# Two attentions on one core: the first segment's output projection in half units with a PSUM bank of their own, and three banks for the maxima

## The chip, the cores and the metric

The kernel runs on one core of a Trainium2 chip. The metric is the device time of one execution in microseconds. The kernel before takes 2726.04 us, the median of three runs (2725.89 to 2726.05).

## What is computed

Two attention layers see the same input `A_x`, 2048 rows of 576 (`B_x` is drawn but not used). A has 32 heads of 18 with keys and values of their own, B has 32 query heads that share one key head and one value head. Their outputs are mixed by a gate per row. All is float32.

```python
x = A_x
g = sigmoid((x * gate_w).sum(-1, keepdims=True))
q, k, v = (x @ A_wqkv).reshape(1, S, 3, H, Dh).transpose(2, 0, 3, 1, 4)   # H = 32, Dh = 18
a = (softmax(q @ k.T * Dh ** -0.5) @ v).transpose(0, 2, 1, 3).reshape(1, S, D) @ A_wo
q = (x @ B_wq).reshape(1, S, H, Dh).transpose(0, 2, 1, 3)
b = (softmax(q @ (x @ B_wk).T * Dh ** -0.5) @ (x @ B_wv)).transpose(0, 2, 1, 3).reshape(1, S, D) @ B_wo
return g * a + (1 - g) * b
```

## The kernel before

**Heads and steps.** The 64 heads (B's 32 first, then A's) are worked through one after the other, each in 16 steps. A step `T` takes one tile of 128 keys against all 2048 queries. The loop at L797 writes out two steps at a time; such a pair is the unit of time in what follows, and a head is eight pairs. Before the loop come the projections (all products that make q, k and v, in split float32), and 11 pairs of lead with negative `T`.

**What a step does.** Scores are `k` times `q` over 54 rows (high and low halves in float16) and two rows that subtract the row maximum; four matmuls of 512 queries each (`step_scores`, L548), in the order strings "sA0" to "sA3" for the first step of the pair and "sB0" to "sB3" for the second. ScalarE turns each into exponentials (L555). One or two steps later `step_pv` (L561) multiplies these by the values and adds into the accumulator `acc`, which has a PSUM bank to itself: "P" or "Q" for all 512 columns of a group, "p", "f", "h", "H" for halves of 256. After a head's last step `head_out` (L571) copies `acc` out with VectorE.

**The maxima.** They are found 22 steps ahead (`LEAD`) by the same product in the other orientation, in other rows of the TensorE array, so a maximum and a score run side by side. Per pair there are eight such matmuls (`step_max`, L511): "mA2", "mA0", "mA3", "mB0" to "mB3", and "x". For "x" the keys' difference of two blocks is used; ScalarE takes its relu (L514), and VectorE adds that to "mA0" of the following pair (L517), which spares "mA1". All the others are reduced by VectorE (L520).

**Order.** The engines run what they are given in program order. `manual_schedule` is on, so the order of the calls is the order of the queues. It is written out by hand in strings, one per kind of pair, L789 to L795:

```python
    PLAIN = "sA0 mA2 sA1 mA0 sA2 mA3 P sA3 mB0 sB0 mB1 sB1 mB2 h sB2 mB3 sB3 x H"
    UNIT = "sA0 mA2 sA1 mA0 sA2 mA3 P sA3 mB0 sB0 mB1 sB1 mB2 U sB2 mB3 sB3 x Q"
    END = "sA0 mA2 sA1 mA3 sA2 mB0 P sA3 mB1 sB0 mA0 sB1 x Q sB2 mB2 sB3 mB3"
    AFTER = "sA0 mA2 p sA1 mA0 sA2 mA3 sA3 x f sB0 mB0 sB1 mB1 h sB2 mB2 sB3 mB3 H"
```

UNIT is taken whenever a unit of the output projection is due; otherwise END where `T` is a multiple of 16, AFTER behind an END, and PLAIN. ALONE stands for the last 11 pairs, which have no maxima left.

**PSUM.** Eight banks: `ps_s` has three for scores, `ps_m` four, `ps_o` one for `acc`. A pool hands its banks out in turn; a tile's first writer waits until the readers of the tile that had the bank are done. `ps_m` serves the maxima (of "x" too), the units of the output projection, half of the projections ahead of the loop, and small transposes.

**The output projection** runs inside the loop, in three segments (`SEG`, L769) of 32 units each. A unit (`out_proj`, L673) is 128 rows by 288 columns: 12 matmuls with four tiles of heads and three products of high and low halves in the first two segments, 3 matmuls in the third. In the first segment ScalarE copies a unit to `oacc` (L683); in the others VectorE adds it (L685). `oih` and `oil`, the normalised heads, are loaded from DRAM by SP's queue, a pair of tiles for four units. The generator yields after each unit, and "U" in the string runs it on by one (`pull`). When units are due is said by `due`: in the first segment by the table `at_ends`, 21 of them at every 16th step from 528 and 11 at every 32nd from 522; in the second, units spread evenly over steps 942 to 1007, about one a pair.

Of the kernel before, what the change touches and what calls it, by code (L numbers as in the profile page):

```python
# [49 lines left out]
def gated_mix_kernel(ctx: ExitStack, tc: tile.TileContext, xT, wall, wv, wo, out):  # L50
# [7 lines left out]
    fixed = ctx.enter_context(tc.tile_pool(name="fixed", bufs=1, side="left"))  # L58
    dram = ctx.enter_context(tc.tile_pool(name="dram", bufs=1, space=DRAM))
    ps_s = ctx.enter_context(tc.tile_pool(name="ps_s", bufs=3, space=PSUM))  # L60
    ps_m = ctx.enter_context(tc.tile_pool(name="ps_m", bufs=4, space=PSUM))
    ps_o = ctx.enter_context(tc.tile_pool(name="ps_o", bufs=1, space=PSUM))
    ctx.enter_context(tc.manual_schedule())

# [19 lines left out]
    ones = fixed.tile([P, 32], F16, name="ones")  # L84
    ones_r = dram.tile([2, S], F16, name="ones_r")
    acc = ps_o.tile([P, 512], F32, name="acc")

    nc.vector.memset(acc, 0.0)
    nc.vector.memset(vb, 1.0)
# [68 lines left out]
    dma(mask_r, mask_d.rearrange("g (m p) -> m g p", p=P), nc.gpsimd)  # L158

    def turn_mask():  # L160
        pt = ps_m.tile([P, 512], F32, name="pm")
        for g in range(4):
            nc.tensor.transpose(pt[:, MT * g:MT * g + MT], mask_r[:, g, :], ident[0:MT, 0:MT])
        nc.vector.tensor_copy(mask, pt[:, 0:4 * MT].rearrange("p (g m) -> p g m", m=MT))
# [28 lines left out]
    def balance(g):  # L193

        r = wpool.tile([P, 2], F32, name="br", bufs=1)
        if g == 0:
            nc.vector.tensor_reduce(r, norm_b, axis=AX.X, op=OP.max)
        else:
            r0 = q_row(H) - 4 * P
            sizes = norm_a[:, r0:r0 + 2 * DH * H].rearrange("p (h a d) -> p a h d", a=2, d=DH)  # L200
            for i in range(2):
                nc.vector.tensor_reduce(r[:, i:i + 1], sizes[:, 1 - i], axis=AX.XY, op=OP.max)
        yield
        pt = ps_m.tile([P, 512], F32, name="pm")
        nc.tensor.transpose(pt[0:2, 0:P], r, ident)
        x = wpool.tile([2, 1], F32, name="bx", bufs=1)
        nc.vector.tensor_reduce(x, pt[0:2, 0:P], axis=AX.X, op=OP.max)
        nc.vector.tensor_scalar(x, x, 1e-18, 1e18, op0=OP.max, op1=OP.min)
        dg = wpool.tile([2, 2], F32, name="bd", bufs=1)
        nc.vector.tensor_scalar(dg, ident[0:2, 0:2], x, None, op0=OP.mult)  # L210
        yield
        pb = ps_m.tile([P, 512], F32, name="pm")
        nc.tensor.matmul(pb[:, 0:2], two, dg, start=True, stop=True)
        b = wpool.tile([P, 2], F32, name="bb", bufs=1)
        nc.vector.reciprocal(b[:, 1:2], pb[:, 1:2])
        nc.vector.tensor_tensor(b[:, 0:1], pb[:, 0:1], b[:, 1:2], op=OP.mult)
        e = wpool.tile([P, 2], I32, name="be", bufs=1)
        nc.vector.tensor_single_scalar(e[:, 0:1], b[:, 0:1].bitcast(I32), 24, op=OP.logical_shift_right)
        nc.vector.tensor_scalar(e[:, 1:2], e[:, 0:1], 1.0, 64.0, op0=OP.mult, op1=OP.add)
        nc.vector.tensor_scalar(e[:, 0:1], e[:, 0:1], -1.0, 190.0, op0=OP.mult, op1=OP.add)  # L220
        t = wpool.tile([P, 2], F32, name="bt", bufs=1)
        nc.vector.tensor_single_scalar(t.bitcast(I32), e, 23, op=OP.logical_shift_left)
        nc.vector.tensor_scalar(t, t, LIFT, None, op0=OP.mult)
        for i in range(2):
            nc.vector.scalar_tensor_tensor(tv, mask[:, g + i, :], t[:, i:i + 1], tv, op0=OP.mult, op1=OP.add)
# [45 lines left out]

    def shared_v(c):
        st = ST.pop(c)
        pv = ps_m.tile([P, 512], F32, name="pm")
        for j in range(4):
            nc.tensor.transpose(pv[:, 18 * j:18 * j + 18],
                                st[ROW_VB:ROW_VB + 18, j * P:(j + 1) * P],
                                ident[ROW_VB:ROW_VB + 18, ROW_VB:ROW_VB + 18])
        nc.vector.tensor_copy(vb[:, 4 * c:4 * c + 4, 0:18],
                              pv[:, 0:72].rearrange("p (j d) -> p j d", d=18))  # L280
# [215 lines left out]

    MX = {}

    def step_max(u, i, c, low=False):

        if u not in MX:
            MX[u] = mxs[u] if u < 2 else mxs[2 + u % 3]
        b = SB if low else MB
        if c == "x":
            k = L["kd", u if u >= H else 0][b:b + 54, :]
        else:
            k = kst(u)[b:b + 54, c * 512:(c + 1) * 512]
        pm = ps_m.tile([P, 512], F32, name="pm")  # L510
        nc.tensor.matmul(pm, qs[u % 3][b:b + 54, i * P:(i + 1) * P], k, start=True, stop=True)  # L511
        if c == "x":
            MX["x", u, i] = lead.tile([P, 512], F32, name="xb", bufs=2)
            nc.scalar.activation(MX["x", u, i], pm, AF.Relu)  # L514
        elif c == 0 and ("x", u, i) in MX:
            junk = lead.tile([P, 512], BF16, name="junk", bufs=1)
            nc.vector.tensor_tensor_reduce(junk, pm, MX.pop(("x", u, i)), 1.0, -3e38, op0=OP.add, op1=OP.max,  # L517
                                           accum_out=MX[u][:, i, c:c + 1])
        else:
            nc.vector.tensor_reduce(MX[u][:, i, c:c + 1], pm, axis=AX.X, op=OP.max)  # L520
# [126 lines left out]
    def out_proj(t0, rows, first=False):  # L647
# [18 lines left out]
        for q in range(8):  # L666
# [3 lines left out]
            for s2 in range(2):  # L670
                st_ = 2 * q + s2
                for hf in range(2):
                    fp = ps_m.tile([P, 512], F32, name="pm")  # L673
                    n = 0
                    for a, b in PRODS:
                        for t, r in enumerate(rows):
                            nc.tensor.matmul(fp[:, 0:288], o[b][:r, t, s2 * P:(s2 + 1) * P],  # L677
                                             w[a][:r, t, 288 * hf:288 * hf + 288],
                                             start=(n == 0), stop=(n == 3 * nt - 1))
                            n += 1  # L680
# [23 lines left out]
    def last_out():  # L704
# [6 lines left out]
        for j in range(4):  # L711
# [1 line left out]
            dma(stk[0:18, cs], oh[32 * j:32 * j + 18, :])  # L713
            dma(stk[18:36, cs], oh[32 * j:32 * j + 18, :])
            dma(stk[36:54, cs], ol[32 * j:32 * j + 18, :])
        pt = ps_m.tile([P, 512], F32, name="pm")
# [7 lines left out]
        yield  # L724
        for st_ in range(16):
            for hf in range(2):
                ps = ps_m.tile([P, 512], F32, name="pm")
# [45 lines left out]
    when(980, lambda: slow.append(prep_last()))  # L773


    at_ends = list(range(528, 849, 16)) + list(range(522, 843, 32))
    assert len(at_ends) == 32

    def due(T, t0, t1, n):
        if t0 == SEG[0][3]:  # L780
            return at_ends.count(T)
        return (n * (T - t0 + 1)) // (t1 - t0) - (n * (T - t0)) // (t1 - t0) if t0 <= T < t1 else 0

    vunits = [(st_, hf) for hf in range(2) for st_ in range(16)]
# [12 lines left out]
    for T in range(-LEAD, NSTEP + 2, 2):  # L797
# [11 lines left out]
        for op in order.split():  # L809
# [6 lines left out]
                if M + 2 < NSTEP:  # L816
                    step_max(*divmod(M + 2, 16), "x")
            elif k in "mM":
                step_max(*divmod(M + second, 16), int(c), k == "M")
            elif k == "s":  # L820
                if T < NSTEP:
                    step_scores(*divmod(T + second, 16), int(c), alone)
# [8 lines left out]
        if slow and M % 16:  # L831
            for _ in range(2 if T > 1000 else 1):
                if slow:
                    try:
                        next(slow[0])
                    except StopIteration:
                        slow.pop(0)
    while slow:
        run(slow.pop(0))
    tail = last_out()  # L840
# [37 lines left out]
```

## Time and profile before

| | us |
|---|---|
| median of three runs (lowest, highest) | 2726.04 (2725.89, 2726.05) |
| the profiled execution | 2726.16 |
| its span in the profile | 2724.3 |
| TensorE busy (matmul) | 2689.0 |
| VectorE busy | 2421.9 |
| ScalarE busy | 2389.5 |
| GpSimd busy | 285.7 |
| mean granted TensorE clock | 0.995 |

Times in the profile are microseconds from the start of the span. A busy TensorE isn't a TensorE at its peak, since matmuls overlap and their ends are modelled. The loop's step 0 has its first exponential at about 307 us; the steps with units of the first segment lie from 1485 to 2262 us, those of the second from 2479 us on.

### The profile page before, as it was taken

What the parts mean: (1) busy time and instruction counts of PE and PEld (TensorE: products, weight loads), DVE (VectorE), ACT (ScalarE), POOL (GpSimd) and SP (SyncE); (2) the same over time, 40 slices, a digit from 0 to 9 for tenths busy, and PEclk for the clock granted to TensorE, in tenths of its full rate; (3) what the DMA queues carried; (4) which work ended last, traced back from release to release, by engine and by line L of the source; (5) the groups of instructions that cost most, each with busy time, mean ns of one, the idle gap of its engine ahead of it and who ended that gap; (6) DMA issues with size and microseconds to landing.
All of it is one profiled execution on the core that took longest, in us unless ns stands there. A gap on an engine that the chain in (4) does not pass through costs nothing.

```text
span 2724.3 us, 57935 instructions
## 1 busy us (share of the span) xinstructions
PE 2689.0 (99%) x22210; PEld 957.2 (35%) x22210; DVE 2421.9 (89%) x4589; ACT 2389.5 (88%) x4809; POOL 285.7 (10%) x531
## 2 busy tenths in 40 slices
PE   8999999999999999999999999999999999999999
PEld 6767522222222222222222333333333332223444
DVE  6335899999999999999999999999999999998865
ACT  4332599999999999999999999999999999998875
POOL 3641000001000200110110001000100021001000
PEclk9999999999999999999999999999999999999998
DMA  6322100002001100110132113112221112122312
GB/s 188 114 97 85 38 16 19 20 22 59 27 18 32 45 26 17 45 43 20 32 72 80 41 49 97 40 41 57 72 66 48 47 58 64 39 68 85 89 36 95
DMA packets 127089, 150.36 MB, mean 55 GB/s; under 512 B 55339, under 2 KB 94411, under 8 KB 125614
## 3 DMA queue, kind: packets, MB, share of 16 engines
q1 hardware_dynamic: 113628, 121.86, 15.8%
q0 software_dynamic: 7968, 19.23, 2.1%
q10 hardware_dynamic: 5216, 5.57, 0.6%
q8 instruction: 174, 2.85, 0.4%
q14 instruction: 103, 0.84, 0.1%
HBM read 90.89 MB, written 46.45 MB: 50 GB/s over the span
## 4 chain that ended last, share of the span: by engine, by line
ACT 50%; PE 40%; DVE 6%; DMA 2%; issue 1%; SPq 1%; POOL 0%; DVEq 0%; ACTq 0%; POOLq 0%
ACT pt L555 45%; PE acc L561 13%; PE ps L548 11%; ACT xb L514 6%; PE pm L677 4%; PE ps L240 4%; PE pm L240 4%; DVE mx L520 3%; PE ps L289 3%; PE pm L511 1%; SPq L56 1%; DMA R<-r_d 1%; DVE oe L571 1%; DVE junk L517 1%; DVE oacc L731 0%
## 5 line engine op out<-in xcount | busy, mean ns | idle before, releaser
L555 ACT ACTIVATE pt<-ps 128x512 f32<-128x512 f32 x4052 | 2093.2, 637 | 67.8 <-PE pm L511 59.8
L520 DVE TENSOR_REDUCE mx<-pm 128x1 f32<-128x512 f32 x3096 | 1941.4, 683 | 93.6 <-PE pm L511 52.8
L548 PE MATMUL ps<-qs,ksb 56*128 56x512 f16 x2688 | 818.4, 380 | 10.7
L511 PE MATMUL pm<-ksb,qs 54*128 54x512 f16 x2364 | 742.2, 383 | 2.2 <-DVE mx L520 1.1
L561 PE MATMUL acc<-pt,vb 128*19 128x512 f32 (+1 forms) x6136 | 592.2, 458 | 1.9
L561 PE MATMUL acc<-pt,vg 128*19 128x256 f32 (+1 forms) x5664 | 579.5, 481 | 2.3 <-DVE oe L571 0.5
L511 PEld LDWEIGHTS <-qs 54*128 54x128 f16 x4096 | 332.2, 93 | 245.6 <-issue 196.7
L548 PE MATMUL ps<-qs,ksa 56*128 56x512 f16 x1364 | 404.3, 379 | 4.8 <-ACT pt L555 1.3
L548 PEld LDWEIGHTS <-ksb 56*128 56x128 f16 x2688 | 175.0, 94 | 622.1 <-issue 575.8
L511 PE MATMUL pm<-ksa,qs 54*128 54x512 f16 x1232 | 384.8, 382 | 0.5 <-ACT xb L514 0.2
L517 DVE CUSTOM_DVE_ANT_0 junk<-pm,xb 128x512 bf16<-128x512 f32 x500 | 340.6, 681 | 0.0
L514 ACT ACTIVATE xb<-pm 128x512 f32<-128x512 f32 x500 | 316.6, 633 | 0.0
L548 PEld LDWEIGHTS <-ksa 56*128 56x128 f16 x1408 | 89.3, 94 | 328.8 <-issue 298.1
L530 POOL TENSOR_SCALAR mt<-mt 128x32 f32<-128x32 f32 x64 | 18.6, 290 | 1612.0 <-DVE mt L528 1612.0
L561 PEld LDWEIGHTS acc<-pt,vb 128*19 128x19 f32 x6136 | 104.1, 96 | 223.5 <-issue 206.4
L561 PEld LDWEIGHTS acc<-pt,vg 128*19 128x19 f32 x5664 | 96.1, 97 | 222.8 <-issue 204.9
L511 PE MATMUL pm<-kdb,qs 54*128 54x512 f16 x372 | 141.5, 380 | 0.0
L248 ACT ACTIVATE ph<-ps,tv 128x512 f16<-128x512 f32 x29 | 19.8, 686 | 67.3 <-PE ps L240 43.2
L292 ACT ACTIVATE vst<-ps 128x288 f32<-128x288 f32 x32 | 13.2, 412 | 67.4 <-PE ps L289 67.4
L571 DVE COPY oe<-acc 128x512 f32<-128x512 f32 x63 | 43.6, 692 | 30.0 <-PE acc L561 27.9
L248 ACT ACTIVATE ph<-pm,tv 128x512 f16<-128x512 f32 x27 | 18.4, 686 | 54.5 <-PE pm L240 40.6
L254 DVE SCALAR_TENSOR_TENSOR pl<-pm,tv,ph 128x512 f16<-128x512 f32 x27 | 20.1, 749 | 48.8 <-ACT ph L248 38.7
(151 smaller groups left out, 1518.6 us busy)
## 6 DMA issues: line engine op xcount, KB each, us to landing
qs<-qkh SPq DMA_DIRECT2D x244, 72.0 KB
qs<-qkl SPq DMA_DIRECT2D x122, 72.0 KB
onh<-oh SPq DMA_DIRECT2D x32, 256.0 KB
onl<-ol SPq DMA_DIRECT2D x32, 256.0 KB
oih<-onh SPq DMA_DIRECT2D x16, 512.0 KB
oil<-onl SPq DMA_DIRECT2D x16, 512.0 KB
ot<-oe SPq DMA_DIRECT2D x220, 36.0 KB
R<-r_d SPq DMA_DIRECT2D x55, 144.0 KB
```

Of the source, the lines that this page charges most:

```text
L240: nc.tensor.matmul(fp[:, a0:b0], w[a][:kr, k, :], X[b][:kr, k, s0 + a0:s0 + b0], start=(n == 0), stop=(n == len(PROJ) - 1), skip_group_che ...
L248: nc.scalar.activation(h, fp, AF.Copy, scale=t)
L289: nc.tensor.matmul(fp[:, 0:288], X[b][:kr, k, st_ * P:(st_ + 1) * P], w[a][:kr, k, :], start=(n == 0), stop=(n == len(PROJ) - 1))
L511: nc.tensor.matmul(pm, qs[u % 3][b:b + 54, i * P:(i + 1) * P], k, start=True, stop=True)
L514: nc.scalar.activation(MX["x", u, i], pm, AF.Relu)
L517: nc.vector.tensor_tensor_reduce(junk, pm, MX.pop(("x", u, i)), 1.0, -3e38, op0=OP.add, op1=OP.max, accum_out=MX[u][:, i, c:c + 1])
L520: nc.vector.tensor_reduce(MX[u][:, i, c:c + 1], pm, axis=AX.X, op=OP.max)
L548: nc.tensor.matmul(ps, kst(u)[b:b + 56, i * P:(i + 1) * P], qs[u % 3][b:b + 56, c * 512:(c + 1) * 512], start=True, stop=True)
L555: nc.scalar.activation(pt, ps, AF.Exp, scale=SCALE / LIFT ** 2)
L561: nc.tensor.matmul(acc[32 * j:32 * j + 19, a:b], v_of(u, i), PT[u, i, j][:, a:b], start=(i == 0 and a == 0), stop=(i == 15), skip_group_ch ...
L571: nc.vector.tensor_copy(oe, acc)
L677: nc.tensor.matmul(fp[:, 0:288], o[b][:r, t, s2 * P:(s2 + 1) * P], w[a][:r, t, 288 * hf:288 * hf + 288], start=(n == 0), stop=(n == 3 * nt ...
```

## The change

- `ps_m` has three banks instead of four; the fourth is a pool of its own, `ps_x`.
- `side()` takes that bank. The units of the first two segments go there, and so do the small transposes ahead of the loop.
- `four()` takes `ps_m` three times and `ps_x` the fourth time. The maxima of the lead (T < 0) use it, and from step 1018 on (`L["tail"]`) the units of the third segment and what comes after the last head. The maxima from step 0 on take `ps_m` alone, and so do the first two scores of a step in the last pairs.
- The generator of the first segment yields once more, after six of a unit's twelve matmuls. Its table, `pieces`, has 64 entries from 524 to 870, 5.5 steps apart on average, for 32 units of two pieces.

```diff
-    ps_m = ctx.enter_context(tc.tile_pool(name="ps_m", bufs=4, space=PSUM))
+    ps_m = ctx.enter_context(tc.tile_pool(name="ps_m", bufs=3, space=PSUM))
+    ps_x = ctx.enter_context(tc.tile_pool(name="ps_x", bufs=1, space=PSUM))
...
+    turn = {"n": 0}
+
+    def side():
+        return ps_x.tile([P, 512], F32, name="px")
+
+    def four():
+
+        turn["n"] += 1
+        return side() if turn["n"] % 4 == 0 else ps_m.tile([P, 512], F32, name="pm")
...
-    def step_max(u, i, c, low=False):
+    def step_max(u, i, c, low=False, lead_on=False):
...
-        pm = ps_m.tile([P, 512], F32, name="pm")
+        pm = four() if lead_on else ps_m.tile([P, 512], F32, name="pm")
...
-                    fp = ps_m.tile([P, 512], F32, name="pm")
+                    fp = four() if "tail" in L else side()
                     n = 0
                     for a, b in PRODS:
                         for t, r in enumerate(rows):
+                            if first and n == 6:
+                                yield
...
-    at_ends = list(range(528, 849, 16)) + list(range(522, 843, 32))
-    assert len(at_ends) == 32
+    pieces = [524 + 11 * i // 4 * 2 for i in range(64)]
 
     def due(T, t0, t1, n):
         if t0 == SEG[0][3]:
-            return at_ends.count(T)
+            return pieces.count(T)
...
-                step_max(*divmod(M + second, 16), int(c), k == "M")
+                step_max(*divmod(M + second, 16), int(c), k == "M", T < 0)
...
+        if T >= NSTEP - 6:
+            L["tail"] = True
```

In `turn_mask`, `balance` and `shared_v` the tile comes from `side()`, in `last_out` from `four()`. By the added lines L548, L555, L511, L514, L520, L561, L571, L677 and L683 become L559, L566, L522, L525, L531, L572, L582, L690 and L696.

TensorE's queue at the start of a plain pair, in a head of B, before. A row gives the line, the operation, the tile written and the tiles read, and the semaphore of the engine waited for; `ps` is a score, `pm` a maximum, `acc` the accumulator:

```order
L548 MATMUL ps_10063<-qs0_92,ksb_95 128x512 [waits Activation_49]
L511 LDWEIGHTS qs1_93
L511 MATMUL pm_10067<-ksb_95,qs1_93 128x512 [waits DVE_49]
L548 LDWEIGHTS ksb_95
L548 MATMUL ps_10071<-qs0_92,ksb_95 128x512 [waits Activation_49]
L511 LDWEIGHTS qs1_93
L511 MATMUL pm_10075<-ksb_95,qs1_93 128x512 [waits DVE_49]
L561 MATMUL acc_100<-pt_9988,vb_97 19x512
```

The same place with the change:

```order
L559 MATMUL ps_10066<-qs0_95,ksb_98 128x512 [waits Activation_49]
L522 LDWEIGHTS qs1_96
L522 MATMUL pm_10070<-ksb_98,qs1_96 128x512 [waits DVE_49]
L559 LDWEIGHTS ksb_98
L559 MATMUL ps_10074<-qs0_95,ksb_98 128x512 [waits Activation_49]
L522 LDWEIGHTS qs1_96
L522 MATMUL pm_10078<-ksb_98,qs1_96 128x512 [waits Activation_49]
L572 MATMUL acc_103<-pt_9991,vb_100 19x512
```

The order of the instructions is the same. The last maximum ahead of `acc` (mA3) waited for VectorE and now waits for ScalarE.

TensorE's queue at a unit of the first segment, before (`woh` and `wol` are the weights' halves, `oih` and `oil` those of the heads):

```order
L548 MATMUL ps_22034<-qs2_94,ksa0_2732 128x512 [waits Activation_49]
L511 LDWEIGHTS qs1_93
L511 MATMUL pm_22038<-ksb_95,qs1_93 128x512 [waits DVE_49]
L677 MATMUL pm_22045<-woh_19342,oih_21768 128x288 [waits DMAHW7_49,DVE_49,Pool_49]
L677 MATMUL pm_22045<-woh_19342,oih_21768 128x288 [waits Pool_49] x3
L677 MATMUL pm_22045<-woh_19342,oil_21770 128x288 [waits DMAHW0_49]
L677 MATMUL pm_22045<-woh_19342,oil_21770 128x288 x3
L677 MATMUL pm_22045<-wol_19343,oih_21768 128x288 x3
L677 MATMUL pm_22045<-wol_19343,oih_21768 128x288 [waits Pool_49]
L548 LDWEIGHTS ksa0_2732
```

With the change, the second piece of a unit:

```order
L559 MATMUL ps_22712<-qs0_95,ksa1_2736 128x512 [waits Activation_49]
L522 LDWEIGHTS qs2_97
L522 MATMUL pm_22716<-ksa0_2735,qs2_97 128x512 [waits DVE_49]
L690 MATMUL px_22496<-woh_19345,oil_21773 128x288 x2
L690 MATMUL px_22496<-wol_19346,oih_21771 128x288 x4
L559 LDWEIGHTS ksa1_2736
```

Twelve matmuls in a row, into a tile of the maxima's banks, are now six, into a tile of `ps_x`.

More of the change, by code (lines that the diff above doesn't have):

```diff
@@ L160, in turn_mask @@
     def turn_mask():
-        pt = ps_m.tile([P, 512], F32, name="pm")
+        pt = side()
         for g in range(4):
@@ L203, in balance @@
         yield
-        pt = ps_m.tile([P, 512], F32, name="pm")
+        pt = side()
         nc.tensor.transpose(pt[0:2, 0:P], r, ident)
@@ L211, in balance @@
         yield
-        pb = ps_m.tile([P, 512], F32, name="pm")
+        pb = side()
         nc.tensor.matmul(pb[:, 0:2], two, dg, start=True, stop=True)
@@ L273, in shared_v @@
         st = ST.pop(c)
-        pv = ps_m.tile([P, 512], F32, name="pm")
+        pv = side()
         for j in range(4):
@@ L715, in last_out @@
             dma(stk[36:54, cs], ol[32 * j:32 * j + 18, :])
-        pt = ps_m.tile([P, 512], F32, name="pm")
+        pt = four()
         for c in range(4):
@@ L726, in last_out @@
             for hf in range(2):
-                ps = ps_m.tile([P, 512], F32, name="pm")
+                ps = four()
                 nc.tensor.matmul(ps[:, 0:288], stk[0:54, st_ * P:st_ * P + P],
```

## The prediction

> **What bounds the kernel now.** I read the page first, then the chain of waits, then the timeline of one pair of steps. The page:
>
> ```profile
> ACT pt L555 45%; PE acc L561 13%; PE ps L548 11%; ACT xb L514 6%; PE pm L677 4%; PE ps L240 4%; PE pm L240 4%; DVE mx L520 3%; PE ps L289 3%; PE pm L511 1%; SPq L56 1%; DMA R<-r_d 1%; DVE oe L571 1%; DVE junk L517 1%; DVE oacc L731 0%
> L555 ACT ACTIVATE pt<-ps 128x512 f32<-128x512 f32 x4052 | 2093.2, 637 | 67.8 <-PE pm L511 59.8
> L520 DVE TENSOR_REDUCE mx<-pm 128x1 f32<-128x512 f32 x3096 | 1941.4, 683 | 93.6 <-PE pm L511 52.8
> ```
>
> 45% of the chain that ended last is the exponential (L555) on ScalarE, 6% the relu (L514) on the same engine. TensorE is 99% busy by the page, but its ends are modelled, so the chain decides. In the middle of a head it runs on ScalarE alone:
>
> ```profile
> 1330.13 0.49 ACT xb L514
> 1330.62 3.92 ACT pt L555 x8
> 1334.54 0.49 ACT xb L514
> 1335.03 3.92 ACT pt L555 x8
> 1338.95 0.49 ACT xb L514
> ```
>
> A pair of steps is nine ScalarE instructions, eight exponentials and a relu: 3.92 + 0.49 = 4.41 us. The relu is the last of a pair. A longer pair therefore needs a loop that passes through ScalarE and is longer than 4.41 us. The timeline of the same pair:
>
> ```profile
> 1334.42 0.61 ACT L514 ACTIVATE xb<-pm 128x512 f32<-128x512 f32 x1
> 1334.59 0.37 PE L548 MATMUL ps<-qs,ksb 56*128 56x512 f16 x1
> 1334.60 0.39 PE L511 MATMUL pm<-ksb,qs 54*128 54x512 f16 x1
> 1334.89 4.05 ACT L555 ACTIVATE pt<-ps 128x512 f32<-128x512 f32 x8
> 1334.91 1.05 PE L561 MATMUL acc<-pt,vb 128*19 128x512 f32 x8
> 1335.90 0.39 PE L548 MATMUL ps<-qs,ksb 56*128 56x512 f16 x1
> 1336.13 0.38 PE L548 MATMUL ps<-qs,ksb 56*128 56x512 f16 x1
> 1336.55 0.37 PE L548 MATMUL ps<-qs,ksb 56*128 56x512 f16 x1
> 1336.56 0.39 PE L511 MATMUL pm<-ksb,qs 54*128 54x512 f16 x1
> 1336.87 0.63 PE L561 MATMUL acc<-pt,vb 128*19 128x256 f32 x8
> 1337.43 0.39 PE L548 MATMUL ps<-qs,ksb 56*128 56x512 f16 x1
> 1337.97 0.63 PE L561 MATMUL acc<-pt,vb 128*19 128x256 f32 x8
> 1338.83 0.61 ACT L514 ACTIVATE xb<-pm 128x512 f32<-128x512 f32 x1
> ```
>
> In the names of the order strings: relu of the last pair (1334.42), sA2 and mA3 side by side (1334.59), P (1334.91), sA3 (1335.90), sB0 (1336.13), sB1 and mB2 (1336.55), h (1336.87), sB2 (1337.43), H (1337.97), relu (1338.83). Two narrower looks at ScalarE give the distance of two exponentials:
>
> ```profile
> 1335.37 1.13 ACT L555 ACTIVATE pt<-ps 128x512 f32<-128x512 f32 x2
> 1335.85 1.14 ACT L555 ACTIVATE pt<-ps 128x512 f32<-128x512 f32 x2
> ```
>
> They start 0.48 apart (1334.89, 1335.37, 1335.85). Nine are 4.30, so a pair has about 0.11 of idle ScalarE, and it lies before the exponential of sB2.
>
> **The three banks.** A maximum waits until the reader of the tile that had its bank is done. With four banks that is the tile four back, with three the tile three back. A plain pair takes tiles in the order A2 A0 A3 B0 B1 B2 B3 x. mA3 is now three behind the x of the pair before, so it waits for that relu. TensorE's queue runs in order, and behind mA3 stand P, sA3 and all later scores. Before, the wait on the relu fell on mB0, which comes after P, long after the relu's end.
>
> What that does: the relu of 1334.42 ends at 1335.03, and mA3 ran at 1334.60, so mA3 comes some 0.49 later, and P and sA3 with it. sA3 has no room: it ran at 1335.90 and its exponential, the fourth of the eight, at 1335.85 + 0.48 = 1336.33, 0.43 behind. The relu of the pair comes after that exponential and four others, and the next mA3 waits for it: a loop of one pair. Its length:
>
> - the relu, 0.61;
> - from the end of a ScalarE instruction to the matmul that waited for it, 0.06: the exponential of 1335.85 with the mean of 637 ns ends at 1336.49, and sB1 waited for it until 1336.55;
> - mA3 to P, 1334.60 to 1334.91: 0.31;
> - P to sA3, 1334.91 to 1335.90: 0.99;
> - sA3 to its exponential: at least the matmul's 0.39, at most the 0.43 seen; I take 0.42;
> - five exponentials to the next relu, 5 x 0.478: 2.39.
>
> Sum 4.78, against 4.41: **+0.37 a pair**. Low end 4.74 (0.03 less for the score, 0.01 of rounding). High end 4.89, if the 0.11 of idle ScalarE ahead of sB2 stays. It should go: that idle arises because sB1 waits from 1336.35 to 1336.55 for an exponential that in the new pair is long done, so sB2 comes 1.53 - 0.20 = 1.33 after sA3, and its exponential could start 1.33 + 0.42 = 1.75 after sA3, while ScalarE gets there at 0.42 + 3 x 0.48 = 1.86. Slack 0.11.
>
> Is another three-bank wait worse? x now waits for the reduce of B1, and H and mA2 stand behind x. That loop is 0.06 + 0.31 + H to sA0 (0.56, 1337.97 to 1338.53, as h to sB2) + 0.42 + four VectorE instructions of 0.60 + a reduce of 0.68 = 4.43. It is shorter than 4.78, so it doesn't decide.
>
> How often: in the program's order 500 maxima now wait for a relu, 446 of them directly ahead of a P; before it was 8. About 30 of the 446 lie in the second segment (below). 416 x 0.37 = **+154 us** (low 416 x 0.33 = 137, high 416 x 0.48 = 200).
>
> The other 54 are in the pairs behind a head's end, where x comes before f and four more exponentials follow its relu. They cost between nothing and 0.37 each, 0 to 20. I take +5, near the bottom, because the relu ends early there.
>
> **The units of the first segment.** One of them now:
>
> ```profile
> 1575.45 0.39 PE L511 MATMUL pm<-ksa,qs 54*128 54x512 f16 x1
> 1575.76 0.56 PEld L677 LDWEIGHTS pm<-woh,oih 128*128 128x128 f32 x4 [0.23 <-issue]
> 1576.79 0.58 PEld L677 LDWEIGHTS pm<-wol,oih 128*128 128x128 f32 x4
> 1577.54 0.39 PE L548 MATMUL ps<-qs,ksa 56*128 56x512 f16 x1
> 1577.64 0.41 ACT L683 ACTIVATE oacc<-pm 128x288 f32<-128x288 f32 x1 [0.78 <-PE pm L677]
> 1577.96 1.09 ACT L555 ACTIVATE pt<-ps 128x512 f32<-128x512 f32 x2
> 1578.08 1.05 PE L561 MATMUL acc<-pt,vg 128*19 128x512 f32 x8
> ```
>
> Twelve matmuls hold TensorE between mB2 (1575.45) and sB2 (1577.54); ScalarE idles 0.78 and then copies the unit out, 0.32 to the next exponential. What a unit costs in all is read from the heads: one copy of acc each.
>
> ```profile
> L571 DVE COPY oe<-acc x32: 691/692/693, 349.7 to 1463.9; 128x512 f32<-128x512 f32 x32
> L571 DVE COPY oe<-acc x22: 691/692/692, 1503.4 to 2298.1; 128x512 f32<-128x512 f32 x22
> ```
>
> Without units a head is (1463.9 - 349.7) / 31 = 35.94; with them (2298.1 - 1503.4) / 21 = 37.84. 21 heads x 1.90 hold 30 of the units, so one costs 1.33, and 32 cost **43**. That goes.
>
> A half unit in its place: weight loads stand (1576.79 - 1575.76) / 8 = 0.129 apart, so six matmuls fewer take 0.77 off. mB2 to sB2 becomes 2.09 - 0.77 = 1.32 where a plain pair has 0.87 (1336.56 to 1337.43): +0.45. Slack 0.11 covers part, so the exponential of sB2 comes 0.34 late. In every second piece the copy (0.32) falls into just this gap: its data are ready 1577.64 - 1575.76 - 0.77 = 1.11 behind the first weight load and so 0.75 + 1.11 = 1.86 behind sA3, just when ScalarE gets there. So both kinds cost about 0.33, a unit 0.66, 32 units **+21** (0 if the gap is absorbed, 43 if halving brings nothing).
>
> Such pairs end in Q instead of H, 0.43 longer. The cover is the relu's wait: sB2 to sA0 is 1.52 there (0.23 + 0.31 + 0.98) and sA0 to mA3 0.47, together 1.99, while the relu releases mA3 at 0.42 + 2 x 0.48 + 0.61 + 0.06 = 2.05 behind sB2. Without that cover it would be 0.43 x 64 = 28. The unit's own bank waits for a copy two pairs old: nothing. The loads of oih and oil on SP's queue keep their number; they now precede the first piece of every fourth unit, and the reads they wait for are a piece's distance old. The q rows behind them in that queue are used two heads (72 us) later, and the queue is held for a piece's distance at most, 2.75 pairs or 13 us. Without the cover each of the eight pairs of loads would hold a head's first score for those 13.
>
> **The second segment** is bound by TensorE:
>
> ```profile
> 2532.86 0.60 ACT L514 ACTIVATE xb<-pm 128x512 f32<-128x512 f32 x1
> 2533.43 0.38 PE L548 MATMUL ps<-qs,ksa 56*128 56x512 f16 x1
> 2533.44 0.38 PE L511 MATMUL pm<-ksb,qs 54*128 54x512 f16 x1
> ```
>
> mA3 at 2533.44 would wait for the relu's end at 2533.46 plus 0.06: 0.08 a pair, 30 pairs, **+3**. The projections, the lead and the tail keep four banks in turn or have a bank aside: 0.
>
> Sum against the profiled execution: 154 + 5 - 43 + 21 + 3 = **+140**. That execution took 2726.16 (span 2724.3) beside the median of 2726.04, so the time is **2866**.
>
> **The rivals.** *The wait is absorbed at the heads' ends.* From the relu before a head's last pair (order END) to the relu of the third pair on there are the loop's parts up to sA3's exponential, 4.78 - 2.39 = 2.39, and then 23 ScalarE instructions; without any idle time 2.39 + 23 x 0.478 = 13.38, which is three pairs of 4.46, hardly more than today. Then a head costs 5 x 4.78 + 13.38 = 37.28, +1.4, 59 heads +83, with the units -43 + 21 and +3: 2790. For it: the two pairs without a wait could catch up. Against it: the catching up must pass TensorE, which has little idle time.
>
> *Faster.* If TensorE came to mA3 at least 0.49 later than now without ScalarE waiting, the bank would be free, and only the units would count: 2726 - 43 + 21 = 2704. For it: the trace has no plain pair where mA3 meets a busy bank. Against it: a later mA3 means a later sA3, and sA3's exponential follows it at 0.43 today, with no room. From 0.01 us of delay on, ScalarE waits.
>
> *The clock falls.* TensorE would now stand still 0.4 us in each pair, and the granted clock could drop:
>
> ```profile
> 1334.90:1339.31 4.41, 4.37 (x42) 1.28 (x40) 4.27 (x10) 4.41 (x11) 0.00 (x0) 1.00 0.01 4
> 2656.00:2672.00 16.00, 14.98 (x137) 3.63 (x138) 2.29 (x4) 14.93 (x32) 0.00 (x0) 1.00 0.07 17
> ```
>
> The last number but two is the granted clock, the second the busy TensorE. At half the clock P alone takes 0.99 more, 446 x 0.99 = +440: 3170 or more. Against it: from 2656 to 2672 TensorE idled 1.02 us in 16 and kept 1.00. The Trainium skill, TensorE: Matmul & The Clock Gate, "A second HAM failure mode: psum-queue depth-cycling", says that idling briefly as a kernel cycles through PSUM banks lets the clock oscillate; by that rule this rival holds. No run here shows it, and the row above speaks against it.
>
> **How the numbers follow.** Forecast, the relu's loop in every plain pair: 0.90. Absorbed at the heads' ends: 0.05. Faster: 0.03. Clock: 0.02. The forecast's own range: low 137 + 0 - 43 + 0 + 2 = +96, high 200 + 20 - 43 + 43 + 5 = +225. The low end has every term low at once, and the high end needs the idle ahead of sB2 to stay, which its slack speaks against, so I go from +106 to +170: **2832 to 2896**. That leaves out the rivals and the outermost tenth of the forecast. A measurement of this kernel tells 0.2% (5.5 us) from no change. Faster by more: 0.03. Within: 0.01. Slower: 0.96.
>
> **What would show it.** In plain pairs the distance of two relus is 4.78; mA3's matmul starts about 0.06 behind the end of the relu before, no longer beside sA2; ScalarE idles about 0.48 ahead of the fourth exponential of a pair and not ahead of the seventh. Heads without units take 38.1 to 38.6. Pairs with a piece take 5.1, and no copy (L683's successor) is preceded by 0.78 of idle time. Wrong it is if mA3 starts beside sA2 at the old distance, if the pairs' length hasn't changed, or if the loss lies at the heads' ends.

## The result, and the profile after

| | before | after |
|---|---|---|
| median, us (lowest, highest), four runs each | 2725.97 (2724.91, 2726.05) | 2868.72 (2868.24, 2869.99) |
| ratio, 95% interval | | 1.0525 (1.0507, 1.0544) |
| profiled execution / its span | 2726.16 / 2724.3 | 2869.08 / 2867.2 |
| TensorE busy (matmul) | 2689.0 | 2833.8 |
| ScalarE busy | 2389.5 | 2429.7 |
| mean granted TensorE clock | 0.995 | 0.994 |

The change makes the kernel 5.25% slower. One execution of the sixth experiment's kernel took 8358.23 us (it is among the four of the median given there): a score's matmul has a mean of 1.03 us in its trace and 0.38 in that of the same kernel's second run, at a mean granted clock of 1.000 and 0.995.

The page of the kernel after: the chain by line, and the two groups whose idle time grew.

```profile
PE acc L572 36%; PE ps L559 34%; PE pm L522 11%; PE px L690 4%; PE ps L251 4%; PE pm L251 3%; PE ps L300 3%; ACT pt L566 1%; DVE mx L531 1%; DVE oacc L744 0%; DVE oacc L698 0%; DVE oe L582 0%; SPq L56 0%; DMA R<-r_d 0%; ACT xb L525 0%
L566 ACT ACTIVATE pt<-ps 128x512 f32<-128x512 f32 x4052 | 2133.6, 621 | 190.9 <-PE pm L522 180.1
L531 DVE TENSOR_REDUCE mx<-pm 128x1 f32<-128x512 f32 x3074 | 1959.8, 684 | 203.6 <-PE pm L522 176.0
```

The exponential held 45% of the chain before and now holds 1%. ScalarE's idle time ahead of the exponentials grew from 67.8 to 190.9 us, VectorE's ahead of the reduces from 93.6 to 203.6, and both mostly end at a maximum (`pm`, L522), since scores and maxima run side by side. Both engines now stand waiting for TensorE, yet TensorE has no more work: it too waits. The chain of waits in the middle of a head (start, length, engine, tile and line) shows where:

```profile
1409.56 0.37 PE pm L522
1409.93 0.99 PE acc L572 x8
1410.92 0.32 PE ps L559
...
1414.37 0.37 PE pm L522
```

Before, the chain stayed on ScalarE here. Now a maximum stands in it alone for 0.37, and then the PV matmuls P for 0.99. The next such maximum comes 1414.37 - 1409.56 = 4.81 later. The chain reports the loop on TensorE's rows, although the loop passes through ScalarE; that shows only in the timeline of the same pair:

```profile
1404.75 0.37 PE L522 MATMUL pm<-ksb,qs 54*128 54x512 f16 x1
1405.05 1.05 PE L572 MATMUL acc<-pt,vb 128*19 128x512 f32 x8
1406.04 0.39 PE L559 MATMUL ps<-qs,ksb 56*128 56x512 f16 x1
1406.46 2.56 ACT L566 ACTIVATE pt<-ps 128x512 f32<-128x512 f32 x5 [0.29 <-PE pm L522]
1408.87 0.64 ACT L525 ACTIVATE xb<-pm 128x512 f32<-128x512 f32 x1
1409.14 0.38 PE L559 MATMUL ps<-qs,ksb 56*128 56x512 f16 x1
1409.56 0.37 PE L522 MATMUL pm<-ksb,qs 54*128 54x512 f16 x1
```

mA3 (1404.75), P (1405.05), sA3 (1406.04), its exponential and four more (1406.46), the relu (1408.87), and the next mA3 at 1409.56, 0.05 behind the relu's end at 1409.51. sA2 ran at 1409.14; mA3 no longer runs beside it.

The copies of `acc` (L582), one a head, for the heads without units and then for those with units of the first segment:

```profile
L582 DVE COPY oe<-acc x32: 691/692/692, 355.3 to 1547.4; 128x512 f32<-128x512 f32 x32
L582 DVE COPY oe<-acc x21: 690/692/693, 1587.7 to 2380.7; 128x512 f32<-128x512 f32 x21
```

(1547.4 - 355.3) / 31 = 38.45 a head, 35.94 before; (2380.7 - 1587.7) / 20 = 39.65, 37.84 before. The first difference is +2.51, the second +1.81. So the loss is made in heads that have no unit at all, and in the heads with units the halving takes part of it back.

The whole span, cut at the heads' first exponentials:

| stretch | before | after | difference |
|---|---|---|---|
| up to head 0 | 307.2 | 310.4 | +3.2 |
| head 0 | 39.4 | 41.6 | +2.2 |
| heads 1 to 31 | 1114.1 | 1192.1 | +78.0 |
| heads 32 to 53 (first segment) | 834.2 | 871.3 | +37.1 |
| heads 54 to 58 | 180.2 | 193.4 | +13.2 |
| heads 59 to 61 (second segment) | 139.7 | 145.3 | +5.6 |
| heads 62 and 63, and the rest | 109.5 | 113.0 | +3.6 |
| span | 2724.3 | 2867.2 | +142.9 |

And one head without units, pair by pair (the first is an END, the second an AFTER, the others are plain):

| | 1 | 2 | 3 | 4 | 5 | 6 | 7 | 8 | head |
|---|---|---|---|---|---|---|---|---|---|
| before | 4.36 | 4.48 | 4.78 | 4.44 | 4.41 | 4.41 | 4.54 | 4.44 | 35.86 |
| after | 4.81 | 4.70 | 4.88 | 4.81 | 4.81 | 4.81 | 4.81 | 4.81 | 38.43 |

### The profile page after: what moved, and what is told of

It reads as the page before. It is cut to its first block, busy times and chain, and to the rows that moved or that the text cites. A ratio compares the mean times of both kernels' runs of the same rounds, so it can differ in the third digit from the quotient of the medians.

```text
span 2867.2 us, 57277 instructions
## 1 busy us (share of the span) xinstructions
PE 2833.8 (99%) x21890; PEld 864.8 (30%) x21890; DVE 2455.2 (86%) x4589; ACT 2429.7 (85%) x4809; POOL 285.6 (10%) x531
## 4 chain that ended last, share of the span: by engine, by line
PE 95%; DVE 2%; ACT 1%; issue 1%; DMA 1%; SPq 0%; DVEq 0%; ACTq 0%
PE acc L572 36%; PE ps L559 34%; PE pm L522 11%; PE px L690 4%; PE ps L251 4%; PE pm L251 3%; PE ps L300 3%; ACT pt L566 1%; DVE mx L531 1%; DVE oacc L744 0%; DVE oacc L698 0%; DVE oe L582 0%; SPq L56 0%; DMA R<-r_d 0%; ACT xb L525 0%
## 5 line engine op out<-in xcount | busy, mean ns | idle before, releaser
L566 ACT ACTIVATE pt<-ps 128x512 f32<-128x512 f32 x4052 | 2133.6, 621 | 190.9 <-PE pm L522 180.1
L531 DVE TENSOR_REDUCE mx<-pm 128x1 f32<-128x512 f32 x3074 | 1959.8, 684 | 203.6 <-PE pm L522 176.0
L522 PE MATMUL pm<-ksb,qs 54*128 54x512 f16 x2342 | 763.5, 380 | 10.1 <-DVE mx L531 1.6
L559 PE MATMUL ps<-qs,ksb 56*128 56x512 f16 x2688 | 764.1, 380 | 0.4
L572 PE MATMUL acc<-pt,vb 128*19 128x512 f32 (+1 forms) x6136 | 592.2, 458 | 0.0
L572 PE MATMUL acc<-pt,vg 128*19 128x512 f32 (+1 forms) x5344 | 571.4, 499 | 0.4 <-DVE oe L582 0.4
L522 PE MATMUL pm<-ksa,qs 54*128 54x512 f16 x1232 | 400.5, 379 | 3.4 <-ACT xb L525 0.4
L559 PEld LDWEIGHTS <-ksb 56*128 56x128 f16 x2688 | 174.9, 94 | 687.2 <-issue 633.0
L559 PE MATMUL ps<-qs,ksa 56*128 56x512 f16 x1364 | 381.4, 380 | 0.6
L525 ACT ACTIVATE xb<-pm 128x512 f32<-128x512 f32 x500 | 314.9, 630 | 0.0
L522 PEld LDWEIGHTS <-qs 54*128 54x128 f16 x4096 | 291.7, 94 | 54.2 <-issue 17.8
L572 PEld LDWEIGHTS acc<-pt,vb 128*19 128x19 f32 x6136 | 104.2, 97 | 405.7 <-issue 384.1
L559 PEld LDWEIGHTS <-ksa 56*128 56x128 f16 x1408 | 89.5, 94 | 356.9 <-issue 319.0
L572 PEld LDWEIGHTS acc<-pt,vg 128*19 128x19 f32 x5344 | 90.6, 97 | 344.6 <-issue 329.7
L522 PE MATMUL pm<-kdb,qs 54*128 54x512 f16 x372 | 139.1, 374 | 1.4 <-DVE mx L531 0.2
L303 ACT ACTIVATE vst<-ps 128x288 f32<-128x288 f32 x32 | 13.2, 412 | 67.4 <-PE ps L300 67.4
L265 DVE SCALAR_TENSOR_TENSOR pl<-ps,tv,ph 128x512 f16<-128x512 f32 x29 | 21.6, 748 | 44.3 <-ACT ph L259 26.3
```

The costliest lines, as they stand in the source:

```text
L265: nc.vector.scalar_tensor_tensor(l, fp, t, h, op0=OP.mult, op1=OP.subtract)
L559: nc.tensor.matmul(ps, kst(u)[b:b + 56, i * P:(i + 1) * P], qs[u % 3][b:b + 56, c * 512:(c + 1) * 512], start=True, stop=True)
L566: nc.scalar.activation(pt, ps, AF.Exp, scale=SCALE / LIFT ** 2)
L572: nc.tensor.matmul(acc[32 * j:32 * j + 19, a:b], v_of(u, i), PT[u, i, j][:, a:b], start=(i == 0 and a == 0), stop=(i == 15), skip_group_ch ...
```

## The experiments

The theory is the prediction's: with three banks mA3 waits for the relu of the pair before, P and sA3 wait behind it in TensorE's queue, and a loop of 4.8 us a pair results. Edits are against the kernel after, unless it says before. A head's length below is that of a head without units, read from its first exponentials; the start is the time up to the first exponential of head 0.

**1. The units whole again, three banks kept.** This tells what the banks cost without the halving.

```diff
-                            if first and n == 6:
-                                yield
...
-    pieces = [524 + 11 * i // 4 * 2 for i in range(64)]
+    pieces = list(range(528, 849, 16)) + list(range(522, 843, 32))
```

> The change without its half units: 32 whole units at their old places, in the side bank; three banks for the maxima stay. Theory (a whole unit costs 1.33, two pieces 0.66 to 0.8 in pairs of 4.81): heads without units stay at 38.43, heads with units grow by 0.5 to 0.7 x 32 / 22, the time is 2885 to 2891. Rival (halving brings nothing, all of the difference in these heads is the banks): 2866 to 2871.

Measured: 2890.18 us (2886.03 to 2891.39), ratio 1.0602 (1.0586, 1.0617). A head takes 38.43, as in the kernel after; heads 32 to 53 take 888.1 instead of 871.3. The halving isn't the cause. With three banks it saves some 16 us, 0.5 a unit. The medians lie 21.5 apart; most of the rest is at the end of the kernel, where this run's granted clock is 0.58 from 2850 to 2860 us and that of the kernel after is 1.00 at the same place.

**2. In addition to that edit, "x" in the bank of its own and the units among the maxima's three banks.** The relu's bank is then used by nothing else, so mA3 no longer waits for the relu, while the maxima still have three banks.

```diff
-        pm = four() if lead_on else ps_m.tile([P, 512], F32, name="pm")
+        pm = four() if lead_on else side() if c == "x" else ps_m.tile([P, 512], F32, name="pm")
...
-                    fp = four() if "tail" in L else side()
+                    fp = four() if "tail" in L else ps_m.tile([P, 512], F32, name="pm")
```

> The side bank goes to x alone; the other seven maxima of a pair and whole units at their old places share the three banks, so no maximum waits for a relu of the pair before. Theory (the wait on the relu ahead of P makes a pair 4.81): pairs return to 4.4 to 4.5, a head without units to 35.9 to 36.3, the time is 2735 to 2770 with some loss in the second segment, where the units stand among the three banks. Rival (it is the number of banks for VectorE's reduces): pairs stay above 4.7 and the time above 2840.

Measured: 2773.76 us (2772.83 to 2775.12), ratio 1.0177 (1.016, 1.0194). Plain pairs are back at 4.40 to 4.44 but for two of 4.99 and 4.71 (4.78 and 4.41 before); a head takes 36.20. So the relu's release of mA3 is the loop: some 116 of the 164 us of the run above go with it. The time is 4 us above what was expected, although that allowed for some loss in the second segment. A pair there takes 6.32, where the kernel before has 5.80, 12.5 us over heads 59 to 61; heads 32 to 53, which have units too, lose 17.0, and heads 1 to 31 10.7. The timeline of this kernel in the second segment, where L688 is the unit:

```profile
2641.16 2.48 DVE L531 TENSOR_REDUCE mx<-pm 128x1 f32<-128x512 f32 x4
...
2642.50 0.79 PE L688 MATMUL pm<-woh,oih 128*128 128x288 f32 x4 [0.23 <-DVE mx L531]
```

With the unit among the maxima in three banks, its first matmul waits for a reduce of VectorE, and sB2 waits behind it.

**3. The transposes of the shared values back among the maxima's banks.** The start had become 3.2 us longer, which the prediction had at nothing. The one bank of `ps_x` was suspected: the second set of transposes (L287) waits there for VectorE's copy of the first.

```diff
     def shared_v(c):
-        pv = side()
+        pv = ps_m.tile([P, 512], F32, name="pm")
```

> The change with one edit: the four transposes of the shared values take a tile of the three banks again instead of the side bank. Theory (the second one waited 2.0 us for the copy out of the first, and the granted clock fell for the matmuls behind it, together 3.15 us ahead of the loop): the first exponential of the loop is back from 310.4 to 307.2 and the time 3 us shorter, 2865 to 2866. Rival (the projections lose this to having three banks): 310.4 and 2868.7 as they are.

Measured: 2871.06 us (2870.29 to 2871.37), ratio 1.0534 (1.0518, 1.0549), with the start 311.4, not shorter. The expectation fell. (The first experiment, which changes nothing ahead of the loop, has a start of 311.4 as well, so the 1.0 over the kernel after says nothing.) TensorE's timeline of this kernel shows why:

```profile
42.70 0.58 PE L287 MATMUL pm<-ident,pst 18*128 18x18 f32 x4 [10.38 <-DVE pd L268]
```

Now the first set finds all three banks held by projections, and TensorE stands 10.38, where the kernel after stands 3.23. This edit put another wait ahead of the one it took away, so it said nothing on the suspicion.

**4. Before, with the units in halves, four banks kept.** ScalarE copies the first six matmuls out, the second six take a new tile, and VectorE adds it. Nothing is held between the pieces.

```diff
-                                             start=(n == 0), stop=(n == 3 * nt - 1))
+                                             start=(n == 0 or first and n == 6), stop=(n == 3 * nt - 1 or first and n == 5))
...
+                            if first and n == 6:
+                                nc.scalar.activation(oacc[:, st_, 288 * hf:288 * hf + 288], fp[:, 0:288], AF.Copy)
+                                yield
+                                fp = ps_m.tile([P, 512], F32, name="pm")
...
+    at_ends = [524 + 11 * i // 4 * 2 for i in range(64)]
```

> The kernel before, four banks in turn, with the pieces of the change: after six matmuls the first half is copied out by ScalarE, the second half goes into a tile of its own and is added by VectorE. Theory (halves cost less TensorE time in a row; VectorE pays 32 adds of 0.37): the heads with units drop from 37.85 to 37.3 to 37.7, the time is 2713 to 2724, heads without units stay at 35.87. Rival (halving costs as much as it brings, as pairs of the order UNIT double): 2726 to 2740.

Measured: 2725.18 us (2724.09 to 2729.0, ten runs), ratio 0.9999 (0.999, 1.0009): no change that can be told, and just outside what the theory expected. Heads 32 to 53 take 832.2, 2.0 less than before and 37.8 each, again just outside, and heads 54 to 58, into which the last two pieces fall, 181.6, 1.4 more. With four banks, halves made in this way, with VectorE's 32 additional adds, are worth next to nothing at this spacing.

**5. The same with another table:** in each head of the segment a piece at its first, third and sixth pair.

```diff
-    at_ends = [524 + 11 * i // 4 * 2 for i in range(64)]
+    at_ends = [16 * h + o for h in range(33, 54) for o in (0, 4, 10)] + [864]
```

> As the run with four banks in turn and each half copied out or added by itself, but with a table that puts the pieces at steps 0, 4 and 10 of each head instead of every 5.5 steps, so that every head's end has one. Theory (a piece at a head's end costs less, as it takes the place of the order END): heads with units 37.3 to 37.7, 2715 to 2723. Rival (the place doesn't matter): 2725.

Measured: 2720.68 us (2719.9 to 2721.7, eleven runs), ratio 0.9982 (0.9973, 0.999). Heads 32 to 53 take 828.6. That is the fastest kernel of the study, 5 us below before, a small gain, but one whose interval leaves out 1. In the run above a head with pieces at its first, fourth and seventh pair takes 37.87, and one with a piece at the second pair in place of the first, the pair behind a head's end, 38.10. This table gives 37.64 in nearly every head. So what halves are worth hangs on where they lie.

**6. P ahead of mA3.** If P's wait behind mA3 were all that matters, the loop would lose mA3 and be shorter; but mA3 then starts 0.99 later, and its bank comes free later.

```diff
-    PLAIN = "sA0 mA2 sA1 mA0 sA2 mA3 P sA3 mB0 sB0 mB1 sB1 mB2 h sB2 mB3 sB3 x H"
-    UNIT = "sA0 mA2 sA1 mA0 sA2 mA3 P sA3 mB0 sB0 mB1 sB1 mB2 U sB2 mB3 sB3 x Q"
+    PLAIN = "sA0 mA2 sA1 mA0 sA2 P mA3 sA3 mB0 sB0 mB1 sB1 mB2 h sB2 mB3 sB3 x H"
+    UNIT = "sA0 mA2 sA1 mA0 sA2 P mA3 sA3 mB0 sB0 mB1 sB1 mB2 U sB2 mB3 sB3 x Q"
```

> The change with one word moved in the orders PLAIN and UNIT: mA3 stands behind P instead of ahead of it, so P no longer queues behind the wait on the relu. If the wait on the relu were all that three banks cost, plain pairs would fall to 4.4 to 4.5. Theory (three banks bind at VectorE too: mB2 has to wait for the reduce of mA3, which now comes P's 0.99 later, and h, sB2 and H stand behind mB2): P to mA3 0.99, mA3 to the end of its reduce 1.2, then h, sB2, x, H and the next four scores 2.7 make a loop of 4.9 to 5.0 a pair, and the time is 2900 to 2990.

Measured: a median of 2988.85 us (2971.12 to 8358.23), ratio 1.0943 (1.0892, 1.0994). The trace is that of the longest execution, so the pairs are read from a second run of the same kernel:

> The same kernel as the run with mA3 behind P, since that run's profile caught an execution of 8358 us in which every matmul was some three times longer. Theory as before: plain pairs of 4.9 to 5.0, and mB2 starts right behind the end of mA3's reduce. If the bank waits are not the cause of 2971, pairs are irregular and mB2 starts beside sB1.

Measured: 2973.71 us (2972.54 to 2974.31), ratio 1.091 (1.0892, 1.0928). Pairs take 4.96, a head 39.52. The timeline of this second run, from one P to the next:

```profile
1430.17 1.05 PE L572 MATMUL acc<-pt,vb 128*19 128x512 f32 x8
1431.15 0.39 PE L522 MATMUL pm<-ksb,qs 54*128 54x512 f16 x1
1431.58 3.08 DVE L531 TENSOR_REDUCE mx<-pm 128x1 f32<-128x512 f32 x5 [0.32 <-PE ps L559]
1432.32 0.37 PE L522 MATMUL pm<-ksb,qs 54*128 54x512 f16 x1 [0.35 <-DVE mx L531]
1432.63 0.63 PE L572 MATMUL acc<-pt,vb 128*19 128x256 f32 x8
...
1435.13 1.05 PE L572 MATMUL acc<-pt,vb 128*19 128x512 f32 x8
```

The wait on the relu is gone and another is there: mA3 runs at 1431.15, its reduce (the first of the five from 1431.58) ends at about 1432.27, and mB2, three tiles on, can start only at 1432.32, with h and sB2 behind it. With three banks there is a loop through VectorE too, and this order makes it the longer one.

**7. Half of P later.** P goes in two halves: "p" ahead of sA2, so that it covers the relu, and "f" behind mB0.

```diff
-    PLAIN = "sA0 mA2 sA1 mA0 sA2 mA3 P sA3 mB0 sB0 mB1 sB1 mB2 h sB2 mB3 sB3 x H"
-    UNIT = "sA0 mA2 sA1 mA0 sA2 mA3 P sA3 mB0 sB0 mB1 sB1 mB2 U sB2 mB3 sB3 x Q"
+    PLAIN = "sA0 mA2 sA1 mA0 p sA2 mA3 sA3 mB0 f sB0 mB1 sB1 mB2 h sB2 mB3 sB3 x H"
+    UNIT = "sA0 mA2 sA1 mA0 p sA2 mA3 sA3 mB0 f sB0 mB1 sB1 mB2 U sB2 mB3 sB3 x Q"
```

> The change with P cut in two in the orders PLAIN and UNIT: its first half stands ahead of sA2, its second behind mB0, so nothing of P lies between mA3 and sA3. Banks, waits and work are the same. Theory (the loop relu, mA3, P, sA3, five exponentials sets the pair): without P's 0.99 the loop is 3.8, below ScalarE's 4.41, and the pair falls to 4.45 to 4.65, what TensorE's additional switch allows; the time is 2770 to 2825. Rival (any order with three banks is held by VectorE's reduces): pairs of 4.75 or more, 2850 or more.

Measured: 2809.81 us (2808.57 to 2810.4), ratio 1.0309 (1.0293, 1.0325). Plain pairs take 4.52 to 4.60, a head 37.10. The timeline of this kernel behind a relu:

```profile
1404.53 0.60 ACT L525 ACTIVATE xb<-pm 128x512 f32<-128x512 f32 x1
1404.67 0.37 PE L522 MATMUL pm<-ksb,qs 54*128 54x512 f16 x1
1404.97 0.63 PE L572 MATMUL acc<-pt,vb 128*19 128x256 f32 x8
1405.53 0.39 PE L559 MATMUL ps<-qs,ksb 56*128 56x512 f16 x1
1405.53 0.39 PE L522 MATMUL pm<-ksb,qs 54*128 54x512 f16 x1
```

Behind mA0 (1404.67) half of P (1404.97) runs while the relu does. mA3 starts beside sA2 at 1405.53, 0.40 behind the relu's end at 1405.13, so it does not wait. The same three banks, with less work between the relu and sA3, lose 59 us less. What makes up the 84 us that are left over the kernel before was not taken apart.

**8. All sets of transposes but the first in a bank of the maxima.** This is the third experiment again, without the wait that spoilt it.

```diff
     def shared_v(c):
-        pv = side()
+        pv = ps_m.tile([P, 512], F32, name="pm") if c else side()
```

> The change with one edit: the first set of transposes of the shared values keeps the side bank, the other three take one of the three banks, which the held projections have left by then. Theory (one bank for the transposes made the second set wait for the first's copy, three held banks made the first set wait in the run where all of them used the three): neither waits, the first exponential of the loop comes at 306 to 308 and the time is 2864 to 2867. Rival (the projections themselves lose by three banks): 310 to 311 and 2868 to 2871.

Measured: 2865.05 us (2864.95 to 2865.8), ratio 1.0512 (1.0497, 1.0528), start 306.5. The relus (L525) of the kernel after and of this one, durations and then first and last start:

```profile
L525 ACT ACTIVATE xb<-pm x500: 597/641/645, 316.3 to 2778.0; 128x512 f32<-128x512 f32 x167
```

```profile
L525 ACT ACTIVATE xb<-pm x500: 597/641/645, 312.5 to 2775.3; 128x512 f32<-128x512 f32 x167
```

The first is 3.8 earlier, and the median 3.7 lower. The start's loss was the second set's wait for the one bank of `ps_x`, with the slower clock behind it (last section).

## Why the prediction was right, step by step

The forecast of 2866 stands against 2868.72, and its sum of +140 against +142.9 in the spans. The sum is closer than its terms, some of which were off in opposite directions.

**The loop.** Right, and shown by the second and seventh experiments: with the relu's bank taken out of the turn, or with half of P moved out from between, the length of 4.81 goes. Its parts in the timeline above: relu 0.64 (0.61 forecast), release 0.05 (0.06), mA3 to P 0.30 (0.31), P to sA3 0.99 (0.99), sA3 to its exponential 0.42 (0.42), five exponentials 1408.87 - 1406.46 = 2.41 (2.39). Sum 4.81 against 4.78. ScalarE's idle time was given as 0.48 ahead of the fourth exponential and reads 0.29: that row counts from the end of the third (1404.54 + 1.63 = 1406.17), while the 0.48 goes by starts, and an exponential overlaps the one ahead of it by 0.16 to 0.19 there. There is none ahead of the seventh, as forecast.

**How often.** Too many. The prediction set 416 maxima outside the second segment directly ahead of a P at 0.37 each, +154. But 42 of the 446 are the mA2 of AFTER pairs, ahead of the half "p", and those pairs belong to the next term; and in heads with pieces UNIT often stands in the place of END or AFTER, which is priced with the pieces below. By heads, the 59 up to the second segment have six such pairs each, at (38.43 - 35.86 - 0.32) / 6 = 0.375: 354 x 0.375 = +133.

**The pairs behind heads' ends.** Mis-sized: +5 forecast, 0.32 x 59 = +19 measured (4.48 to 4.70 and 4.78 to 4.88 in the table of pairs). The prediction took a value near the bottom of its range of 0 to 20 because "the relu ends early there", and priced one wait, that of mB2 for the relu of the same pair. The timeline of the kernel after shows two others:

```profile
1393.53 0.62 ACT L525 ACTIVATE xb<-pm 128x512 f32<-128x512 f32 x1
1394.14 1.88 DVE L531 TENSOR_REDUCE mx<-pm 128x1 f32<-128x512 f32 x3
1394.20 0.37 PE L522 MATMUL pm<-ksb,qs 54*128 54x512 f16 x1
1394.50 0.63 PE L572 MATMUL acc<-pt,vb 128*19 128x256 f32 x8
...
1396.07 0.37 PE L522 MATMUL pm<-kdb,qs 54*128 54x512 f16 x1
1396.37 0.63 PE L572 MATMUL acc<-pt,vb 128*19 128x256 f32 x8
```

mA2 waits for the relu (end 1394.15, start 1394.20) with "p" behind it, and "x" at 1396.07 follows the last of the three reduces, which ends at 1396.02, with "f" (1396.37) behind it. The wait that was priced isn't there: that relu ends at 1397.57, and mB2 starts beside sB2 at 1398.14.

**The whole units.** 43 forecast; the heads 32 to 53 before hold 834.2 - 22 x 35.87 = 45 over heads without units, 1.41 a unit.

**The pieces.** 0.66 a unit forecast, +21. Measured 871.3 - 22 x 38.43 = 25.8 for the 62 pieces in these heads, which is 0.42 a piece, 0.83 a unit, and 27 in all. Rows of ScalarE's timeline in the kernel after, behind a first piece, and then behind a second piece with its copy (L696):

```profile
1601.40 1.08 ACT L566 ACTIVATE pt<-ps 128x512 f32<-128x512 f32 x2 [0.17 <-PE pm L522]
```

```profile
1615.81 0.43 ACT L696 ACTIVATE oacc<-px 128x288 f32<-128x288 f32 x1
1616.11 1.11 ACT L566 ACTIVATE pt<-ps 128x512 f32<-128x512 f32 x2
```

Behind the first piece ScalarE idles 0.17 ahead of sB2's exponential. Behind the second the copy falls into that gap, as the prediction had it, and the 0.78 of idle time ahead of it is gone. Most pairs with a piece inside a head take 5.15 to 5.20 (5.1 forecast) and the next 4.72 to 4.81, so such a piece costs 0.27 to 0.39; some pairs take 5.25 to 5.37. The missing part lies mostly around heads' ends, where 15 of the 62 pieces fall. A piece at the second pair of a head makes it 5.55 and the next 4.72, against 4.70 and 4.88: 0.69. One at the first pair gives 5.17, 5.00 and 4.77 against 4.81, 4.70 and 4.88: 0.55. The prediction had priced all 64 from a plain pair.

**The second segment.** 0.08 a pair forecast, 6.03 - 5.80 = 0.23 measured, +7 instead of +3. A wait was overlooked. The timeline of the kernel after:

```profile
2723.47 0.60 ACT L525 ACTIVATE xb<-pm 128x512 f32<-128x512 f32 x1
2724.04 0.38 PE L559 MATMUL ps<-qs,ksb 56*128 56x512 f16 x1
2724.13 0.37 PE L522 MATMUL pm<-ksa,qs 54*128 54x512 f16 x1
...
2725.27 1.29 DVE L531 TENSOR_REDUCE mx<-pm 128x1 f32<-128x512 f32 x2
2725.86 0.38 PE L559 MATMUL ps<-qs,ksb 56*128 56x512 f16 x1
2726.01 0.37 PE L522 MATMUL pm<-ksa,qs 54*128 54x512 f16 x1
```

mA3 comes 0.09 behind sA2, for the relu, as forecast. mB2 comes 0.15 behind sB1: it has mA3's bank, whose reduce, the first of the two from 2725.27, ends just ahead of it. 0.09 and 0.15 are the 0.23.

**The start.** Forecast at nothing, because the small transposes "have a bank aside". One bank aside means that each set waits for the copy of the one before: +3.2, shown by the eighth experiment.

Together 133 + 19 - 45 + 27 + 7 + 3 = +144, about the +142.9 of the spans. The 21 too many of the loop, and 2 too few of the whole units, were made up by 14 too few at the heads' ends and 13 too few for the pieces, the second segment and the start.

**The rivals.** *Absorbed at the heads' ends* would have had the three pairs there at 4.46; they took 4.81, 4.70 and 4.88. *Faster* would need mA3 to come late of itself; it waits in every plain pair. *The clock falls*: the row of the windows view over 100 us of the kernel after (length, then busy time and count of TensorE, weight loads, VectorE, ScalarE and GpSimd, then the granted clock, the DMA share and GB/s):

```profile
1400.00:1500.00 100.00, 99.38 (x836) 22.18 (x834) 93.95 (x177) 93.91 (x188) 18.50 (x25) 1.00 0.24 55
```

The clock is 1.00. TensorE's queue stands for a bank in each pair, but TensorE itself is busy for 99.38 of the 100 us, with modelled ends: sA2 (1409.14 to 1409.52) runs through nearly all of mA3's wait (to 1409.56), so by these rows the 0.4 us of standing still that this rival needed is hardly there. The section on psum-queue depth-cycling in TensorE: Matmul & The Clock Gate, the page of the Trainium skill that the prediction named, lets the clock oscillate where TensorE idles briefly as it cycles through PSUM banks. No run here puts that to the test.

**What stays open.** The cause of the one execution of 8358.23 us was not found. A kernel with four banks for the maxima and one more for the pieces was not tried: the eight banks are all taken.

## What to carry to other kernels

Before a bank is taken out of a rotation, write down for each tile which reader now releases its bank, and what stands behind the waiting instruction in its in-order queue; where that work leads back to the same reader, add up the loop and compare it with the present period. A fraction of a microsecond there is paid in every round (0.38 in 4.4 us here), while the gain it was meant for came 32 times. And price a piece of work from the kinds of pairs it will fall on, not from the plainest: the same half unit cost 0.27 in one place and 0.69 in another.

## What the runs showed of the hardware

TensorE's clock fell after a short stop. In the start of the kernel after, TensorE waits 1.95 us for `ps_x`, and the windows view shows the granted clock (third number from the end) halved in the 3.4 us behind it:

```profile
43.40:46.80 3.40, 1.45 (x8) 0.78 (x8) 2.32 (x5) 3.35 (x8) 3.15 (x7) 1.00 0.63 210
46.80:50.20 3.40, 3.40 (x9) 2.62 (x9) 2.99 (x6) 2.95 (x5) 3.38 (x6) 0.50 0.46 154
```

9 matmuls ran in it, where the kernel of the last experiment, without the stop, has 15 at a clock of 1.00:

```profile
46.80:50.20 3.40, 3.40 (x15) 2.35 (x14) 3.10 (x5) 3.30 (x6) 3.38 (x7) 1.00 0.46 154
```

So 1.95 us of standing still in one place cost about 1.4 us more in clock, an estimate from 6 matmuls fewer and the 3.40 / 15 = 0.23 that one takes. The kernels of the first and seventh experiments stand at the same place, for 2.26 and 1.49 us, and their clock in the same 3.4 us is 0.50 and 0.60.

The relu's duration also grew, from a median of 613 ns to the 641 of the row above. The same view of the kernel before:

```profile
L514 ACT ACTIVATE xb<-pm x500: 597/613/717, 312.6 to 2637.7; 128x512 f32<-128x512 f32 x167
```

The relu starts as far behind the instruction ahead of it as before, 0.48; its duration goes with how long ScalarE has run without a pause. Taken one by one, the five exponentials from 1406.46 on, behind 0.29 of idle time, last 0.60, 0.59, 0.60, 0.62 and 0.63, and the relu behind them 0.64, although they start 0.48 to 0.50 apart: each overlaps the one ahead of it a little more. In the kernel before (1338.83), and in the second segment (2723.47), the relu is the third instruction behind a pause, and takes 0.61 and 0.60. A longer run of ScalarE without a pause thus put the relu's end, on which mA3 waits, 0.03 later.
